# Second layer: a small copy that holds GpSimd's residues behind each routing comparison, and VectorE's residues behind a round's operations

## The chip, the cores and the metric

The kernel runs on one core of one Trainium2 chip. The metric is device time in microseconds (us), the median of several runs. The core has TensorE (PE in the profile, with its weight loads apart as PEld), VectorE (DVE), ScalarE (ACT), GpSimd (POOL) and SyncE (SP, which issues most DMAs). Each engine works its own queue in order; engines wait for each other through semaphores.

## The reference, cut to what matters

Attention with a window makes a matrix x of 3072 rows of 512. A first layer of eight experts follows, and then the second layer, where the change lies. It assigns every row to one of eight experts so that each expert gets 384 rows, then runs the expert's two matrix products:

```python
logits = x @ w_gate
order = np.argsort(-logits.flatten())
for idx in order:
    tok, e = int(idx) // E, int(idx) % E
    if assigned[tok] >= 0 or counts[e] >= cap:   # cap = 3072 // 8 = 384
        continue
    assigned[tok] = e
    counts[e] += 1
out[mask_e] = np.maximum(x[mask_e] @ w1[e], 0.0) @ w2[e]
```

## The kernel before, in words

**The routing.** `Route.steps` doesn't sort. It makes eight picks, k = 0 to 7; each finds the expert that fills next, the score at which it is full, and its 384 rows. A pick of k below 7 runs three or four rounds of a search that narrows the threshold some sixty-fold each time. A round is a chain over two engines. VectorE writes `ub`, then the comparison `cmp` (128 x 1792 numbers, bf16) of all scores with 64 thresholds, then the small numbers `b0` and `b1` (columns of the tile `sc`). TensorE counts the result in 13 small matmuls into the PSUM tile `rt` (L1682). VectorE turns the counts into `gsm` and `gg`, TensorE sums `gg` in one matmul (L1965), and VectorE takes the maximum (`J8m`) and two small operations on `sc`, which start the next round's `ub`. After a pick's last round, VectorE and TensorE (tiles `ohb`, `ft`, `rc`, `pj`) make the list `idx` of the pick's rows, and GpSimd gathers these rows from DRAM (`xg`, three indirect DMAs), followed by a copy of the expert's number (`em`).

**The experts.** `Ffn.run` works the eight picks' experts one after the other, each in eight blocks of the hidden width, 64 blocks in all. Numbers are split in a high part and a residue, so that a product is three matmuls. ScalarE makes the high parts (`w1h`, `w2h`, `hh`, `xh`), and a subtraction makes the residues: `w1l` of the first weights (on VectorE for even blocks, on GpSimd for odd ones), `w2l` of the second weights (always on GpSimd in this layer), `hl` and `xl` on VectorE from PSUM. A block is 12 matmuls into `ph` (L1030) and, two blocks later, nine into `y` (L950). The rows of the next expert are transposed (`tr`, L796) in the blocks 6 and 7 of the one before; `tr` has a single buffer, so that a transposition waits until `xl` of the one before has been read from it. The residues are asked for some blocks ahead: `w1l` three, `w2l` two.

**What sets the order.** The order is written out. In every block `side(q)` is called four times, q = 0 to 3: it issues one of the four splits (0 and 1: the high part and the residue of `w2`; 2 and 3: those of `w1`) and the transpositions that are due, and then calls `tick()`. `tick()` lets the routing (`rt.pop`) issue its next piece if the planner's clocks allow it, and asks for weights and gathers. So the pieces of a routing round come behind a split in each engine's queue.

**The copy that is already there.** In pick 1 alone, GpSimd copies `b0` (one number) to the tile `hold` after each round but the first (L1945 and L1946). Nothing reads `hold`. GpSimd's next instruction starts when the copy is done, and the copy waits for `b0`, which VectorE writes behind the comparison. VectorE writes `b0` of the next round only when the copy has read the one before.

Of the kernel before, what the change touches and what calls it, by code (L numbers as in the profile page):

```python
# [10 lines left out]
F32 = mybir.dt.float32  # L11
# [47 lines left out]
def bc(ap, shape):  # L59
    return ap.to_broadcast(shape)  # L60


class K:
    def __init__(self):
        self.clk = Clock()
# [714 lines left out]
class Ffn:  # L780
# [42 lines left out]
    def run(self, js, w1, w2, src, yout, hook=None, xp=((6, 0), (6, 2), (7, 0), (7, 2)), LEAD=3, LAG=2, pre=None, onx=None, more=(), mark=lambda s, n: None):  # L823
# [5 lines left out]
        total = 8 * len(js)  # L829
# [37 lines left out]
        def poll_w(n, ws=(0, 1)):  # L867
            for _ in range(n):
                for i in ws:
                    w = want[i]  # L870
                    if w and 4 * (w[0] - 1) <= done[i] and (src.ready_e2 if w[0] % 2 else src.ready_e)(alljs[w[0] // 2]):
                        load(i, w.pop(0))
# [19 lines left out]
        def split2(c, part):  # L892
            r, q = need(1, c), c % 4
            if part == 0:
                ch[1][c] = (wk.tile([128, 512], F32R, name="w2h", bufs=W2B),
                            wk.tile([128, 512], F32R, name="w2l", bufs=W2B))
                nc.scalar.activation(ch[1][c][0], r[q // 2][:, q % 2, :] if isinstance(r, list) else r[:, q, :], AF.Copy)  # L897
            else:
                h, lo = ch[1][c]
                eng = nc.vector if self.vsplit or small(c) and c % 2 else nc.gpsimd  # L900
                eng.tensor_tensor(lo, r[q // 2][:, q % 2, :] if isinstance(r, list) else r[:, q, :], h.bitcast(F32), op=OP.subtract)  # L901
                done[1] = c + 1
# [22 lines left out]
        def split(s, part):  # L925
            if part < 2:
                if s in w2at:
                    split2(w2at[s], part)
            elif s + LEAD < total:
                split1(s + LEAD, part - 2)  # L930
# [11 lines left out]
        def tick():  # L942
            if hook is not None:
                hook()
            poll_w(2)
            poll_x()
# [10 lines left out]
        late = []  # L957
# [31 lines left out]
        for s in range(last + 1):  # L989
# [3 lines left out]
            def side(q):  # L993
                while q == 3 and late:
                    split(*late.pop(0))
                if q == 1 and late:
                    late.append((s, 1))
                else:
                    split(s, q)
                if jx + 1 < len(js) and s < total:  # L1000
                    for d in range(4):
                        if xp[d] == (f, q):
                            prep(js[jx + 1], d)
                tick()

            if s < total and small(s):
                q = f % 4
# [453 lines left out]
JC, NIT, FEW, IDLE = 64, 4, 2, (3, 2, 1)  # L1461
# [83 lines left out]
class Route(Src):  # L1545
# [4 lines left out]
    def __init__(self, nc, g, pool, xs):  # L1550
        self.nc, self.g, self.p, self.xs = nc, g, pool, xs
        self.e, self.regs, self.idx, self.x = {}, {}, {}, {}
        self.gen = self.steps()
        self.comp = []
        self.em3 = {}
        self.at = [0.0, 0.0]
        p = pool
        self.L = p.tile([128, NR, E], F32, name="L")
        self.LG = p.tile([128, NSUB, E], F32, name="LG")
        self.ent = p.tile([128, NSUB, 2], I32, name="ent")  # L1560
        self.pn = p.tile([128, NMAIN], F32, name="pn")
        self.vb = p.tile([128, NMAIN], BF, name="vb")
        self.tki = p.tile([128, 3, NMAIN], I32, name="tki")
        self.S_ = p.tile([128, NR], F32, name="S_")
        self.OH = p.tile([128, NR, E], BF, name="OH")
        self.ub = p.tile([128, NR], BF, name="ub")
        self.cmp = p.tile([128, 2, JC, HR], BF, name="cmp")
        self.cuts = ((0, HA), (HA, HT + 1))
        self.cmp2 = [p.tile([128, 2, JC, e - o], BF, name=f"cmp{o}") for o, e in self.cuts]
        self.T = p.tile([128, NR], F32, name="T_")  # L1570
        self.sc = p.tile([128, 20], F32, name="sc")
        self.fl = p.tile([128, E], F32, name="fl")
        self.lb = p.tile([128, E], F32, name="lb")
        self.pad = p.tile([128, SSML], F32, name="pad")
        self.pw = p.tile([128, NIT], F32, name="pw")
        self.dd1 = p.tile([128, 4, NIT], F32, name="dd1")
        self.hold = p.tile([1, 2], F32, name="hold")
        self.of = p.tile([2, 128], F32, name="of")
        self.z = p.tile([128, 64], BF, name="z")
        self.tm = p.tile([128, NR], F32, name="tm")  # L1580
        self.chk = p.tile([128, 3, E], F32, name="chk")
        self.want = p.tile([128, 3, E], F32, name="chw")
        (self.lo0, self.lo, self.lop, self.b0, self.b1, self.J, self.esum, self.eidx, self.bad, self.t0, self.nbig, self.span,
         self.half, self.nrow, self.hi, self.J2, self.nv) = (self.sc[:, i:i + 1] for i in range(17))
# [318 lines left out]
    def steps(self):  # L1903
        nc, g, p = self.nc, self.g, self.p
# [15 lines left out]
        for k in range(E):  # L1920
# [4 lines left out]
            if k < E - 1:  # L1925
# [4 lines left out]
                for it in range(first, last + 1):  # L1930
                    d, inv = dd[:, 0, it:it + 1], dd[:, 1, it:it + 1]
                    if k == 0:
                        if it > first:
                            V.scalar_tensor_tensor(self.ub, bc(dd[:, 2, it - 1:it], [128, NR]), J, self.T, op0=OP.mult, op1=OP.add)
                            self.against(V)
                            V.scalar_tensor_tensor(lo, J, dd[:, 0, it - 1:it], b0, op0=OP.mult, op1=OP.add)
                        if it < last:
                            V.tensor_scalar(b1, dd[:, 3, it:it + 1], lo, None, op0=OP.add)
                            V.tensor_scalar(self.T, S_, b1, dd[:, 1, it + 1:it + 2], op0=OP.subtract, op1=OP.mult)
                        if it == first:  # L1940
                            V.tensor_scalar(b0, d, -1.5, lo, op0=OP.mult, op1=OP.add)
                    else:
                        self.compare(V, slice(0, 2), slice(0, HR), inv)
                        V.tensor_scalar(b0, d, -1.5, lo0 if it == 0 else lo, op0=OP.mult, op1=OP.add)
                        if k == 1 and it > 0:  # L1945
                            nc.gpsimd.tensor_copy(self.hold[:, it - 1:it], b0[0:1])  # L1946
                        if it < last:
                            V.tensor_scalar(b1, dd[:, 0, it + 1:it + 2], -128.0, b0, op0=OP.mult, op1=OP.add)
                    if k == 0 and it == first + 1:
                        z = self.z  # L1950
                    self.fill((0 if k == 0 else WT[7] if k == 1 else WT[0]) if it == first else WT[9 if it == first + 2 else 0] if k == 0 else WT[8])
                    yield clk.dve + CM[min(k, 2)]
                    self.count(pn, range(HT + 1), k == 0 and it > first)
                    clk.mm(64 * (HT + 1))
                    if it == first:
                        nc.tensor.matmul(pc, g.ones, OH, start=True, stop=True, skip_group_check=True)
                        nc.scalar.activation(junk, pc, AF.Copy, accum_out=chk[:, 0, k:k + 1])
                    gg = p.tile([JC, E], BF, name="gg")
                    V.tensor_scalar(gs, pn[JC:2 * JC, E:2 * E], -1.0, float(CAP) - 0.5, op0=OP.mult, op1=OP.add)
                    V.tensor_tensor(gg, pn[0:JC, 0:E], gs, op=OP.is_ge)  # L1960
                    if k == 0 and it > first:
                        V.tensor_scalar(b0, d, -1.5, lo, op0=OP.mult, op1=OP.add)
                    self.fill(WT[1])
                    yield clk.dve + 0.2
                    nc.tensor.matmul(pb, g.ones[0:JC, :], gg, start=True, stop=True, skip_group_check=True)  # L1965
                    V.max(J8, pb)
                    if k == 0 and it == first + 1:
                        nc.tensor.matmul(self.cbank[0:64, 0:64], z, z, start=True, stop=True, skip_group_check=True)
                    if k > 0:
                        if it < last:  # L1970
                            V.scalar_tensor_tensor(lop, J, d, b1, op0=OP.mult, op1=OP.add)
                        V.scalar_tensor_tensor(lo, J, d, b0, op0=OP.mult, op1=OP.add)
# [297 lines left out]
```

## Time and profile before

| | |
|---|---|
| median of 3 runs (lowest to highest) | 872.02 us (867.66 to 873.99) |
| the profiled execution | 868.5 us, of which 866.8 us are its span |
| TensorE busy in the span | 824.1 us (95%) |
| VectorE, ScalarE, GpSimd busy | 612.3, 385.3, 343.3 us |
| mean granted TensorE clock | 0.982 |

The span goes from the first to the last instruction of one execution; times in rows count from its start. The second layer's matmuls begin at 523 us. TensorE is the engine that is nearly always busy, so that its waits and its clock decide the end; the other engines count where TensorE waits for them.

### The profile page before, as it was taken

Reading aid. Unit: us, or ns where it says so; the run is one execution under the profiler, and the core shown is the slowest. Engines: PE = TensorE matmul, PEld = TensorE weight load, DVE = VectorE, ACT = ScalarE, POOL = GpSimd, SP = SyncE. Lnnn points to the kernel's source line nnn. Section 1 sums busy time; section 2 is a strip of 40 time slices with the busy share of each in tenths; the row PEclk is TensorE's granted clock in tenths of the full one; section 3 lists DMA queues with packets and bytes.
Section 4 is the critical chain, followed back from the end, with each engine's and each line's share of the span. In section 5 each row is a group of like instructions: output and inputs, shape, how many; then the busy total and the mean of one; then the engine's idle time right before and its main releaser. Section 6 shows DMA issues by size and latency. Waiting matters only on the chain.

```text
span 866.8 us, 15190 instructions
## 1 busy us (share of the span) xinstructions
PE 824.1 (95%) x5006; PEld 657.6 (76%) x5006; DVE 612.3 (71%) x1760; ACT 385.3 (44%) x1091; POOL 343.3 (40%) x560
## 2 busy tenths in 40 slices
PE   8889999989999999999999988999999898999997
PEld 4666666667888888888888647787888787889995
DVE  6888787866679696969694578776868687753310
ACT  5667777754343434343433213343434252434441
POOL 5456958664230101010000014437374445375562
PEclk9999999999999999999999979999999898999999
DMA  7434645747354535343348125434433444255411
GB/s 214 161 113 142 148 147 147 231 161 215 96 166 126 171 122 164 103 150 119 122 146 309 42 78 180 159 134 134 134 134 135 134 134 135 98 169 172 138 44 42
DMA packets 70655, 122.85 MB, mean 142 GB/s; under 512 B 9890, under 2 KB 24102, under 8 KB 70440
## 3 DMA queue, kind: packets, MB, share of 16 engines
q1 hardware_dynamic: 63848, 102.36, 37.4%
q0 software_dynamic: 6720, 19.43, 7.1%
q8 instruction: 42, 0.69, 0.3%
q14 instruction: 45, 0.37, 0.2%
HBM read 102.06 MB, written 19.71 MB: 140 GB/s over the span
## 4 chain that ended last, share of the span: by engine, by line
PE 75%; DVE 14%; ACT 4%; issue 4%; POOL 1%; DMA 0%; POOLq 0%; DVEq 0%; ACTq 0%
PE ph L1030 27%; PE y L950 27%; PE sp L323 4%; PE po L395 3%; ACT P L352 3%; PE rt L1682 2%; PE tr L796 2%; DVE w1l L922 2%; PE pt L360 2%; PE rc L1517 1%; DVE sc L145 1%; PE px L431 1%; DVE mx L342 1%; DVE cmp L145 1%; PE sp L409 1%
## 5 line engine op out<-in xcount | busy, mean ns | idle before, releaser
L1040 ACT ACTIVATE hh<-ph 128x384 fp32r<-128x384 f32 (+1 forms) x112 | 60.2, 538 | 276.2 <-PE ph L1030 275.6
L1030 PE MATMUL ph<-xh,w1h 128*128 128x384 f32 (+1 forms) x448 | 168.9, 377 | 0.1
L1030 PE MATMUL ph<-xh,w1l 128*128 128x384 f32 (+1 forms) x448 | 162.9, 364 | 2.3 <-DVE w1l L922 2.3
L1030 PE MATMUL ph<-xl,w1h 128*128 128x384 f32 (+1 forms) x448 | 162.1, 364 | 0.0
L950 PE MATMUL y<-w2h,hh 128*128 128x512 f32 x384 | 155.2, 404 | 0.0
L950 PE MATMUL y<-w2h,hl 128*128 128x512 f32 x384 | 151.2, 394 | 0.0
L950 PE MATMUL y<-w2l,hh 128*128 128x512 f32 x384 | 151.2, 394 | 0.0
L1041 DVE SCALAR_TENSOR_TENSOR hl<-ph,hh 128x384 fp32r<-128x384 f32 (+1 forms) x112 | 68.7, 613 | 104.6 <-ACT hh L1040 103.7
L901 POOL TENSOR_TENSOR w2l<-w2r,w2h 128x512 fp32r<-128x512 f32 x60 | 78.0, 1306 | 76.5 <-ACT w2h L897 53.3
L1195 POOL DMA_INDIRECT xg<-xd,ent x26 | 27.8, 1070 | 195.9 <-DMA ent<-idtab 190.6
L1219 DVE SCALAR_TENSOR_TENSOR junk<-yr,wgb 128x512 f32<-128x512 f32 x160 | 103.5, 690 | 0.0
L1030 PEld LDWEIGHTS ph<-xh,w1l 128*128 128x128 f32 x448 | 85.6, 191 | 12.6 <-DVE w1l L922 3.0
L1030 PEld LDWEIGHTS ph<-xh,w1h 128*128 128x128 f32 x448 | 85.7, 191 | 12.0 <-issue 1.7
L352 ACT ACTIVATE P<-sp,mx 128x132 f32<-128x132 f32 x192 | 69.3, 369 | 50.4 <-DVE mx L342 18.0
L1030 PEld LDWEIGHTS ph<-xl,w1h 128*128 128x128 f32 x448 | 85.3, 191 | 7.6
L950 PEld LDWEIGHTS y<-w2h,hl 128*128 128x128 f32 x384 | 72.5, 189 | 15.8
L950 PEld LDWEIGHTS y<-w2h,hh 128*128 128x128 f32 x384 | 73.3, 191 | 11.6
L950 PEld LDWEIGHTS y<-w2l,hh 128*128 128x128 f32 x384 | 72.9, 190 | 11.6
L323 PE MATMUL sp<-kr,qs 64*128 64x260 f32 (+1 forms) x384 | 58.9, 404 | 13.5 <-ACT P L352 12.3
L917 ACT ACTIVATE w1h<-w1r 128x512 fp32r<-128x512 f32 x108 | 67.4, 624 | 3.0 <-DVE lp L449 2.1
L922 DVE TENSOR_TENSOR w1l<-w1r,w1h 128x512 fp32r<-128x512 f32 x78 | 66.5, 853 | 2.4 <-ACT w1h L917 2.4
L897 ACT ACTIVATE w2h<-w2r 128x512 fp32r<-128x512 f32 x108 | 67.6, 626 | 0.0
(392 smaller groups left out, 1398.9 us busy)
## 6 DMA issues: line engine op xcount, KB each, us to landing
w1r<-in_w_dram SPq DMA_DIRECT2D x29, 1024.0 KB, 5.5
w2r<-in_w_dram SPq DMA_DIRECT2D x29, 1024.0 KB, 5.8
vr<-in_v_dram SPq DMA_DIRECT2D x16, 384.0 KB, 4.8
xd<-xb SPq DMA_DIRECT2D x16, 384.0 KB, 3.3
xs<-yr SPq DMA_DIRECT2D x24, 256.0 KB, 5.6
kr<-in_kT_dram SPq DMA_DIRECT2D x15, 396.0 KB, 4.4
qr<-in_qT_dram SPq DMA_DIRECT2D x15, 384.0 KB, 4.8
wgb<-in_wg2T_dram SPq DMA_DIRECT2D x1, 2048.0 KB, 8.9
```

The lines of the kernel that those rows point to most:

```text
L323: nc.tensor.matmul(sp[:, hd, c0:260], qs[o:o + 64, 128 * i:128 * i + 128], kr[o:o + 64, k0:k0 + 260 - c0], start=True, stop=True)
L352: nc.scalar.activation(z.P[:, n % 2, hd, :], s.sp[:, hd, 128:260], AF.Exp, bias=s.mx[:, hd:hd + 1], accum_out=z.sm[:, n % 2, hd:hd + 1])
L897: nc.scalar.activation(ch[1][c][0], r[q // 2][:, q % 2, :] if isinstance(r, list) else r[:, q, :], AF.Copy)
L901: eng.tensor_tensor(lo, r[q // 2][:, q % 2, :] if isinstance(r, list) else r[:, q, :], h.bitcast(F32), op=OP.subtract)
L917: nc.scalar.activation(h, v, AF.Copy)
L922: eng.tensor_tensor(lo, v, h.bitcast(F32), op=OP.subtract)
L950: nc.tensor.matmul(o, l, r, start=(first and i == 0), stop=(end and i == 2))
L1030: nc.tensor.matmul(ph, wp[:, c, :], xp_[:, c, 0:NTK], start=(d == 0 and i == 0), stop=(d == 3 and i == len(cut[d]) - 1))
L1040: nc.scalar.activation(hh, ph, AF.Relu)
L1041: nc.vector.scalar_tensor_tensor(hl, ph, 0.0, hh.bitcast(F32), op0=OP.max, op1=OP.subtract)
L1195: self.nc.gpsimd.indirect_dma_start(out=self.xg[j][:, a, :], out_offset=None, in_=self.G.xd[0:k, :], in_offset=bass.IndirectOffsetOnAxis(a ...
L1219: nc.vector.scalar_tensor_tensor(junk, yr[:, 0:DM], 1.0, wgb[:, e, :], op0=OP.mult, op1=OP.mult, accum_out=lg[:, e:e + 1])
```

## The change

Picks 2 to 6 get the copy too: each round but a pick's first one ends with GpSimd's copy of `b0` to `hold`, which are 14 copies more. And in the second layer, `side(3)` of a block calls `tick()` ahead of its split when that split is one for VectorE (an even `w1` block); the pieces of the routing that this tick issues then stand ahead of `w1l` in the queues.

```diff
             def side(q):
                 while q == 3 and late:
                     split(*late.pop(0))
+                ticked = q == 3 and not self.vsplit and s + LEAD < total and (s + LEAD) % 2 == 0 and not late
+                if ticked:
+                    tick()
                 if q == 1 and late:
                     late.append((s, 1))
                 else:
...
                         if xp[d] == (f, q):
                             prep(js[jx + 1], d)
-                tick()
+                if not ticked:
+                    tick()
...
-        self.hold = p.tile([1, 2], F32, name="hold")
+        self.hold = p.tile([1, NIT], F32, name="hold")
...
                         V.tensor_scalar(b0, d, -1.5, lo0 if it == 0 else lo, op0=OP.mult, op1=OP.add)
-                        if k == 1 and it > 0:
+                        if it > 0:
                             nc.gpsimd.tensor_copy(self.hold[:, it - 1:it], b0[0:1])
```

GpSimd's queue in pick 5, before (`xg` are the gathers of expert 4's rows, the residues those of blocks 26 to 31; pick 6 has the same sequence one expert later, before and now):

```order
L901 TENSOR_TENSOR w2l<-w2r,w2h 128x512
L1882 DMA xg_9009<-xs,idx_9005 128x512 x3
L1885 COPY em_9013<-em 1x1
L922 TENSOR_TENSOR w1l<-w1r,w1h 128x512
L901 TENSOR_TENSOR w2l<-w2r,w2h 128x512 x2
L922 TENSOR_TENSOR w1l<-w1r,w1h 128x512
```

and now:

```order
L901 TENSOR_TENSOR w2l<-w2r,w2h 128x512
L1886 DMA xg_9020<-xs,idx_9016 128x512 x3
L1889 COPY em_9024<-em 1x1
L1950 COPY hold<-sc 1x1
L922 TENSOR_TENSOR w1l<-w1r,w1h 128x512
L901 TENSOR_TENSOR w2l<-w2r,w2h 128x512
L1950 COPY hold<-sc 1x1
L901 TENSOR_TENSOR w2l<-w2r,w2h 128x512
L922 TENSOR_TENSOR w1l<-w1r,w1h 128x512
L1950 COPY hold<-sc 1x1
L901 TENSOR_TENSOR w2l<-w2r,w2h 128x512 x2
```

Three copies have come in: the second one stands between the two `w2l` that followed each other, the third ahead of the pair after that. VectorE's and TensorE's queues are the same before and now in picks 5 and 6.

VectorE's queue in pick 3, where blocks 11 and 12 run, before:

```order
L145 TENSOR_TENSOR ohb<-iob,rb 128x1792
L922 TENSOR_TENSOR w1l<-w1r,w1h 128x512
L145 MEMSET pj 128x2
L145 TENSOR_SCALAR gsm<-rt 64x8
L145 TENSOR_TENSOR gg<-rt,gsm 64x8
L1041 SCALAR_TENSOR_TENSOR hl<-ph,hh 128x384
L145 TENSOR_REDUCE pj<-rc 128x2x3
L145 SCALAR_TENSOR_TENSOR idx_7467<-pj 128x3
L145 SCALAR_TENSOR_TENSOR idx_7469<-pj 128x3
L145 MAX J8m<-rt 128x8
```

and now:

```order
L145 TENSOR_SCALAR gsm<-rt 64x8
L145 TENSOR_TENSOR gg<-rt,gsm 64x8
L922 TENSOR_TENSOR w1l<-w1r,w1h 128x512
L145 MAX J8m<-rt 128x8
L145 SCALAR_TENSOR_TENSOR sc<-J8m,dd,sc 128x1 x2
L145 TENSOR_SCALAR ub<-S__77,sc,dd 128x28
L145 TENSOR_TENSOR cmp<-ub,iou 128x1792
L145 TENSOR_SCALAR sc<-dd,sc 128x1 x2
L1045 SCALAR_TENSOR_TENSOR hl<-ph,hh 128x384
L145 TENSOR_REDUCE pj<-rc 128x2x3
L145 SCALAR_TENSOR_TENSOR idx_7481<-pj 128x3
```

The residue of block 14 stands behind `gg` instead of ahead of it, and the second round's comparison has moved ahead of the row list (`pj`, `idx`) that the gathers read. GpSimd's queue at the same place, before:

```order
L901 TENSOR_TENSOR w2l<-w2r,w2h 128x512 x2
L1882 DMA xg_7471<-xs,idx_7467 128x512 x3
L1885 COPY em_7475<-em 1x1
L922 TENSOR_TENSOR w1l<-w1r,w1h 128x512
L901 TENSOR_TENSOR w2l<-w2r,w2h 128x512 x2
```

and now:

```order
L901 TENSOR_TENSOR w2l<-w2r,w2h 128x512
L1950 COPY hold<-sc 1x1
L901 TENSOR_TENSOR w2l<-w2r,w2h 128x512
L922 TENSOR_TENSOR w1l<-w1r,w1h 128x512
L1886 DMA xg_7505<-xs,idx_7481 128x512 x3
L1889 COPY em_7509<-em 1x1
L1950 COPY hold<-sc 1x1
```

The three gathers, which followed two `w2l`, now follow a copy, a `w2l` and a `w1l`. VectorE's order differs besides in one residue of pick 1 (block 6, which moves behind the second `ohb`) and in pick 4, where two residues and the rounds around them change places; TensorE's order differs in picks 3 and 4 alone, and that of the SP queue nowhere.

## Rows read from the trace of the kernel before

**Rows 1.** Section 1 of the page: TensorE's busy time and share.

```profile
PE 824.1 (95%) x5006; PEld 657.6 (76%) x5006; DVE 612.3 (71%) x1760; ACT 385.3 (44%) x1091; POOL 343.3 (40%) x560
```

**Rows 2.** TensorE's waits, 515 to 867 us: total us, times, longest.

```profile
PE rt L1682 <- DVE cmp L145: 5.6, 2, 3.0
PE tr L796 <- DVE xl L798: 3.2, 3, 1.8
...
PE rc L1517 <- DVE pj L145: 0.5, 1, 0.5
```

**Rows 3.** Timeline, VectorE in pick 5: start, duration, instruction.

```profile
674.76 4.14 DVE L922 TENSOR_TENSOR w1l<-w1r,w1h 128x512 fp32r<-128x512 f32 x1
...
679.02 2.33 DVE L145 SCALAR_TENSOR_TENSOR sc<-J8m,dd,sc 128x1 f32<-128x1 f32 x2
...
681.60 1.09 DVE L145 TENSOR_TENSOR cmp<-ub,iou 128x1792 bf16<-128x1792 bf16 x1
```

**Rows 4.** Timeline, GpSimd at the same place.

```profile
674.59 1.28 POOL L922 TENSOR_TENSOR w1l<-w1r,w1h 128x512 fp32r<-128x512 f32 x1
675.83 2.52 POOL L901 TENSOR_TENSOR w2l<-w2r,w2h 128x512 fp32r<-128x512 f32 x2
678.84 1.28 POOL L922 TENSOR_TENSOR w1l<-w1r,w1h 128x512 fp32r<-128x512 f32 x1 [0.49 <-ACT w1h L917]
```

**Rows 5.** Timeline, VectorE in a round of pick 3 with GpSimd issuing gathers.

```profile
592.66 0.17 DVE L145 MAX8 J8m<-rt 128x8 f32<-128x8 f32 x1 [0.46 <-PE rt L1965]
...
593.47 1.09 DVE L145 TENSOR_TENSOR cmp<-ub,iou 128x1792 bf16<-128x1792 bf16 x1
```

**Rows 6.** Chain that ended last: start, us, what (picks 4, 5 and 6).

```profile
625.71 0.78 PE rt L1682 x13
...
627.78 1.27 PE ph L1030 x6
...
636.10 2.08 PE y L950 x9
...
688.16 2.32 PE y L950 x9
...
734.56 2.95 PE y L950 x9
```

**Rows 7.** Stretches; the number behind the five engines is the granted clock.

```profile
596.00:604.00 8.00, 6.24 (x42) 4.96 (x41) 6.59 (x13) 2.69 (x6) 6.03 (x6) 1.00 0.64 199
...
682.00:689.00 7.00, 6.25 (x30) 5.62 (x31) 4.06 (x13) 0.81 (x2) 0.00 (x0) 0.53 0.38 146
```

**Rows 8.** Timeline, VectorE in pick 6.

```profile
721.56 3.63 DVE L922 TENSOR_TENSOR w1l<-w1r,w1h 128x512 fp32r<-128x512 f32 x1
```

**Rows 9.** Timeline, VectorE and TensorE in pick 2.

```profile
561.88 0.96 DVE L145 SCALAR_TENSOR_TENSOR sc<-J8m,dd,sc 128x1 f32<-128x1 f32 x2
...
565.07 0.55 PE L796 MATMUL tr<-cst,xg 128*128 128x128 f32 x3 [0.64 <-DVE xl L798]
```

**Rows 10.** Timeline, GpSimd's gathers and TensorE's transpositions, picks 2 and 3.

```profile
551.44 0.96 POOL L1882 DMA_INDIRECT xg<-xs,idx  x1 [0.30 <-issue]
...
555.21 0.33 PE L796 MATMUL tr<-cst,xg 128*128 128x128 f32 x1 [0.49 <-DMA xg<-xs,idx]
...
592.40 0.99 POOL L1882 DMA_INDIRECT xg<-xs,idx  x1 [0.63 <-DVE idx L145]
593.69 1.70 POOL L1882 DMA_INDIRECT xg<-xs,idx  x1 [0.30 <-issue]
...
603.79 0.55 PE L796 MATMUL tr<-cst,xg 128*128 128x128 f32 x3 [1.76 <-DVE xl L798]
```

**Rows 11.** Timeline at a copy of pick 1: GpSimd, VectorE, TensorE.

```profile
527.53 0.17 POOL L1946 COPY hold<-sc 1x1 f32<-1x1 f32 x1 [1.68 <-DVE sc L145]
...
527.85 1.65 DVE L922 TENSOR_TENSOR w1l<-w1q,w1h 128x512 fp32r<-128x512 f32 x1
...
529.55 0.45 PE L1030 MATMUL ph<-xh,w1l 128*128 128x384 f32 x1 [1.12 <-DVE w1l L922]
```

## The prediction

> **What bounds the kernel now.** I read the page first: TensorE is busy 824.1 us, 95% of the span [rows 1]. So only its waits and its clock can shorten the time, and the change touches the second layer alone. The view of TensorE's waits from 515 us on shows how little there is: two waits of 5.6 us together for a routing comparison (3.0 and 2.6), three of 3.2 us together for `xl`, and some of half a microsecond [rows 2]. The windows show what belongs to the first two: the granted clock was 0.53 of full speed in the 7 us behind the longer one, while it stayed at 1.00 around the wait of 1.76 us at 603.8 [rows 7, 10]. So the two long waits cost twice, once idle and once at 1.2 instead of 2.4 GHz.
>
> The timeline shows where they come from. In pick 5 VectorE starts a `w1l` at 674.76, takes 4.14 us for it, then 2.33 us for two operations on one number per partition, and the comparison ends at 681.60 + 1.09 = 682.69 [rows 3]. GpSimd runs residues back to back at that very time, one from 674.59 and two until 675.83 + 2.52 = 678.35, then more from 678.84 on [rows 4]. VectorE's residue ends some 0.6 us behind GpSimd's third. Nobody else was late: an undisturbed round takes 593.47 + 1.09 - 592.66 = 1.90 us from the maximum to the comparison's end [rows 5]. VectorE's operations on SBUF stand still while GpSimd works through its residues, and TensorE's count waits for the comparison. Pick 6 is the same with a residue of 3.63 us [rows 8].
>
> **Pick 5, the first term.** The copies put a stop into GpSimd's queue: residue, residue, copy, residue, residue, copy. The first copy stands behind the gathers, while VectorE writes its `b0`, and waits for nothing; it moves GpSimd's first residue by its own length, 0.17 us [rows 11]. From 674.59 + 0.17 GpSimd works two residues (1.28 + 1.26 from rows 4) until 677.3, and then must wait at the second copy for a `b0` that VectorE has yet to write. VectorE is free at 677.3. Its residue needs some 0.6 us more (678.90 behind 678.35 in rows 3 and 4), so 677.9; the undisturbed round of 1.90 us puts the comparison's end at 679.8 instead of 682.7. TensorE was due there at 682.75 - 3.0 = 679.7. A wait of 0.1 us is left of 3.0: **-2.9 us**. If VectorE wins the race at 674.8 and GpSimd's two come behind its residue, they end at 678.0, and the two small operations start then: the comparison ends near 679.6, the same.
>
> With no long wait the clock should not fall. What the fall cost is read off the chain: at full clock, the count and the 12 matmuls behind it took 627.78 + 1.27 - 625.71 = 3.34 us and nine `y` matmuls 2.08 [rows 6]. In pick 5 the same two pieces took 688.16 - 682.75 = 5.41 and 2.32. That is **-2.3 us**.
>
> **Pick 6** has the same queue: the wait of 2.6 us goes whole (GpSimd's two residues end near 723.6, the comparison near 726.2, TensorE is due at 726.5), **-2.6 us**. The slow clock there lasted longer, 2.07 us in the first piece as above and 2.95 - 2.08 = 0.87 in the second [rows 6], **-2.9 us**.
>
> **Picks 1 and 2.** In pick 2 a `w2l` of GpSimd stands behind the first of the new copies, so it can't stretch VectorE's two small operations to 0.96 us, against 0.35 undisturbed; the 0.6 us saved bring `xl` forward and end the wait of 0.64 us [rows 9]: **-0.6 us**. In pick 1 a `w1l` has moved behind the second `ohb`, for which TensorE waited half a microsecond [rows 2]: **-0.5 us**.
>
> **Pick 3, where the change also costs.** The 1.76 us wait for `xl` [rows 10] came from a `w1l` that stood in front of a comparison, and goes. But the gathers of expert 2's rows now stand behind a copy, a `w2l` and a `w1l`, and the list they read behind one more comparison. Worked forward on before's clock: GpSimd's three residues ahead of the copy end near 590.6 and hold VectorE's small operations up to there, the comparison of the second round ends at 592.4 to 592.8, the copy is through at 593.0, the two residues at 595.6 (1.28 each), and VectorE's `idx`, two SBUF operations, may wait for them until 596.0. Three gathers 1.29 us apart (592.40 to 593.69) end at 599.6, and rows land 2.8 us behind the last (555.21 against 551.44 + 0.96) [rows 10]: 602.4. TensorE, which reads them in block 14, is due between 600.2 and 601.5, after up to 1.3 us of waiting for `gg` on the same count. So 1.9 to 2.2 us of new waits replace 1.76: I take **+0.3 us**. Bounds: nothing new at all, -1.8; the gathers one more residue late and a clock fall like that of pick 5 behind it, +1.3 + 2.3 = +3.6.
>
> At this place a rule and a row differ. The second gather took 1.70 us instead of 0.99 while VectorE ran the comparison of 1.09 us [rows 5, 10]. The Trainium skill (SBUF — State Buffer, Who interferes with whom) says that an operation on two SBUF tensors takes only the read side of the ports that VectorE shares with GpSimd, while writing DMA descriptors needs the write side, so the comparison should not have slowed the gather. By the rule the price here would be 0.3 us; should the next comparison slow a gather by the row's 0.7 us, it would be 1.0.
>
> **The rest.** The 14 copies are 14 x 0.17 = 2.4 us of GpSimd, which is 40% busy [rows 1]; they lie beside TensorE's work. Residues held back come up to some 4 us later. They are asked for two or three blocks ahead, a block lasts some 4.2 us (12 matmuls and nine), and no row of TensorE's waits names GpSimd; so 8 us cover 4, at nothing. Behind the third copy of picks 5 and 6 GpSimd's pair now runs against VectorE's next `w1l`, with `gsm`, `gg` and an `xl` queued behind it; by the same reckoning `xl` is just in time: **+0.2 us** for the two, up to +1.3 each if one more residue comes between. Moving the tick ahead of the split adds no instruction; its effect is in picks 1, 3 and 4 above, and pick 4 comes out at nothing within 0.3 us.
>
> **The sum** is -2.9 - 2.3 - 2.6 - 2.9 - 0.6 - 0.5 + 0.3 + 0.2 = -11.3 us. The profiled execution took 868.5 us, so 857.2. Its own before lies 3.5 us under the median of the three runs, 872.02; I take the difference off the median: **860.7 us**. One per cent, 8.7 us, is about what a measurement of this kernel can tell from no change, since the three runs span 6.3 us.
>
> **Rivals.**
>
> The gain is half: the waits of picks 5 and 6 go, but a clock fall stays, because pick 3's wait grows or because a fall hits another weak place. Two falls of the kind in picks 5 and 6 are 2.3 + 2.9 = 5.2 us: -11.3 + 5.2 = -6.1, 866 us, within 1%. For it: the two long waits are not the only ones, and the new one of pick 3 stands beside a count of small matmuls as theirs did. Against it: the wait of 1.76 us was followed by a clock of 1.00 [rows 7, 10].
>
> The copy doesn't hold what matters: the stall may come from the residues in front of the copy, which it leaves where they are. In pick 5 two of three remain ahead of it, and if VectorE needs much longer than 0.6 us to get through behind them, say one GpSimd residue more (1.28 us), a wait of 1.4 us stays in each pick; with the clock staying up, the gain is 11.3 - 2.6 = 8.7 us, 863 us, on the edge of 1%.
>
> The other side: slower. In pick 1, the copy that exists lets GpSimd loose exactly behind the comparison, at 527.53; its `w1l` stretches VectorE's `w1l` to 1.65 us, and TensorE waits 1.12 us for that [rows 11]. If each of the 14 new copies does this, it is 14 x 1.12 = 15.7 us against 11.3: +4.4, 876 us. It decides from 10 of 14 on. For it: VectorE's even residues now stand right behind the round, where GpSimd's start. Against it: pick 1 is the start of the layer, with the residue needed at once; later VectorE's residues are asked for three blocks, 12 us, ahead. The Trainium skill (SBUF — State Buffer, Who interferes with whom) has the rule behind it, that the order of issue decides which of the two blocks the other. The rows agree, 674.59 ahead of 674.76 in pick 5 and 527.53 ahead of 527.85 in pick 1 [rows 3, 4, 11].
>
> **How the numbers follow.** Forecast as worked out (855 to 862.5): 0.58. Copy holds too little (about 863): 0.17. Clock falls stay (about 866): 0.18, with up to 870. Slower by the copies' collisions: 0.04, and 0.03 for no effect at all. The low end is the sum with pick 3 at its good bound (-1.8 for +0.3), 858.6, and as much of the scatter of the runs before, 4.4 us below their median, as chance should leave: 855. The high end takes in the clock falls: 867. Faster by over 1% (under 863.3): 0.68; within 1%: 0.28; slower: 0.04.
>
> **What the profile after would show.** In pick 5 and 6, `w1l` on VectorE takes about 3.1 and 2.5 us, not 4.14 and 3.63; the two small operations behind it 0.35; the count follows with a wait under 0.3 us; the granted clock of both stretches is 1.00. In pick 3 the wait for `xl` is gone and one for `xg` of about a microsecond stands in block 14. GpSimd waits at 14 more copies, and no matmul waits for GpSimd. The prediction is wrong if the comparisons of picks 5 and 6 still end over 1 us late, if the clock falls at new places, or if waits for `w1l` of VectorE appear behind the copies.

## The result, and the profile after

The changed kernel takes 856.56 us (median of six runs, 855.23 to 861.10), against 870.24 us for the kernel before in the same comparison (six runs, 867.66 to 873.99): a ratio of 0.9844, with a 95% interval of 0.9813 to 0.9874. The forecast was 860.7 us in a range of 855 to 867, and faster. The profiled execution took 855.23 us against 868.5, 13.3 us less where the sum of the prediction had 11.3.

Section 1 of the page of the changed kernel, as in [rows 1]:

```profile
PE 818.0 (96%) x5001; PEld 654.6 (77%) x5006; DVE 609.3 (71%) x1760; ACT 385.1 (45%) x1091; POOL 347.5 (41%) x574
```

TensorE's waits of the changed kernel in the second layer, as in [rows 2]: total us, times, longest.

```profile
PE ph L1034 <- DVE w1l L922: 1.1, 1, 1.1
PE tr L796 <- DMA xg<-xs,idx: 0.8, 1, 0.8
...
PE rt L1686 <- DVE cmp L145: 0.5, 2, 0.2
```

The 5.6 us for `cmp` have become 0.5, and `xl`, with 3.2 us in [rows 2], is no longer in the list. No wait names GpSimd. The one for `w1l` is that of pick 1, which was there before [rows 11].

The timeline of VectorE in pick 5 after, to be read against [rows 3]:

```profile
672.97 0.67 DVE L922 TENSOR_TENSOR w1l<-w1r,w1h 128x512 fp32r<-128x512 f32 x1
...
674.34 2.43 DVE L145 SCALAR_TENSOR_TENSOR sc<-J8m,dd,sc 128x1 f32<-128x1 f32 x2
...
677.01 1.09 DVE L145 TENSOR_TENSOR cmp<-ub,iou 128x1792 bf16<-128x1792 bf16 x1
```

GpSimd at the same place, against [rows 4]:

```profile
674.09 1.28 POOL L922 TENSOR_TENSOR w1l<-w1r,w1h 128x512 fp32r<-128x512 f32 x1
675.33 1.29 POOL L901 TENSOR_TENSOR w2l<-w2r,w2h 128x512 fp32r<-128x512 f32 x1
678.29 0.17 POOL L1950 COPY hold<-sc 1x1 f32<-1x1 f32 x1 [1.67 <-DVE sc L145]
678.43 1.28 POOL L901 TENSOR_TENSOR w2l<-w2r,w2h 128x512 fp32r<-128x512 f32 x1
```

GpSimd works its two residues until 676.62, VectorE's small operations are through at 676.77, and the third residue waits 1.67 us at the copy instead of standing in their way. The comparison ends at 678.10. TensorE's count in pick 5, before and now:

```profile
682.75 0.95 PE L1682 MATMUL rt<-OH,cmp 128*128 128x16 bf16 x13 [3.01 <-DVE cmp L145]
...
678.16 0.96 PE L1686 MATMUL rt<-OH,cmp 128*128 128x16 bf16 x13 [0.21 <-DVE cmp L145]
```

It has waited for 0.21 us instead of 3.01. Pick 6 shows the same with `w1l` at 2.26 us (it was 3.63, [rows 8]), and there no wait is left.

Stretches of the changed kernel; the number behind the five engines is the granted clock, as in [rows 7]:

```profile
593.00:598.00 5.00, 5.00 (x20) 4.38 (x19) 2.88 (x10) 0.91 (x2) 4.23 (x7) 0.66 0.56 176
...
676.00:683.00 7.00, 6.79 (x42) 5.55 (x41) 5.71 (x17) 2.81 (x6) 3.65 (x6) 1.00 0.58 165
683.00:690.00 7.00, 7.00 (x48) 5.94 (x47) 4.34 (x11) 2.73 (x6) 4.58 (x4) 1.00 0.36 138
720.00:727.00 7.00, 7.00 (x52) 6.14 (x52) 4.65 (x12) 1.53 (x3) 4.98 (x5) 1.00 0.63 226
```

Behind the counts of picks 5 and 6 the clock stays at 1.00, where it was 0.53 in pick 5. There is one new fall, in pick 3 (0.66).

Where the time went is read from the start of each block's first matmul, before and after. The difference is -1.8 us at block 28, -6.75 at block 30 (pick 5), the same at block 36, -12.3 at block 38 (pick 6), and -12.3 from there to the last block.

### The profile page after: what moved, and what is told of

Its sections match the earlier page's. It is cut to its first block, busy times and chain, and to the rows that moved or that the text cites. A ratio compares the mean times of both kernels' runs of the same rounds, so it can differ in the third digit from the quotient of the medians.

```text
span 853.5 us, 15197 instructions
## 1 busy us (share of the span) xinstructions
PE 818.0 (96%) x5001; PEld 654.6 (77%) x5006; DVE 609.3 (71%) x1760; ACT 385.1 (45%) x1091; POOL 347.5 (41%) x574
## 4 chain that ended last, share of the span: by engine, by line
PE 78%; DVE 10%; ACT 5%; issue 4%; POOL 2%; DMA 0%; POOLq 0%; DVEq 0%; ACTq 0%
PE ph L1034 29%; PE y L950 28%; PE sp L323 4%; PE po L395 3%; ACT P L352 3%; PE tr L796 2%; PE rt L1686 2%; PE pt L360 2%; PE rc L1521 2%; PE px L431 1%; DVE mx L342 1%; DVE cmp L145 1%; PE sp L409 1%; DVE sc L145 1%; DVE sp L340 1%
## 5 line engine op out<-in xcount | busy, mean ns | idle before, releaser
L1034 PEld LDWEIGHTS ph<-xh,w1l 128*128 128x128 f32 x448 | 84.8, 189 | 12.3 <-DVE w1l L922 3.0
L323 PE MATMUL sp<-kr,qs 64*128 64x260 f32 (+1 forms) x384 | 59.1, 405 | 13.3 <-ACT P L352 12.0
L922 DVE TENSOR_TENSOR w1l<-w1r,w1h 128x512 fp32r<-128x512 f32 x78 | 62.9, 806 | 2.4 <-ACT w1h L917 2.4
```

What stands on the lines that cost most here:

```text
L323: nc.tensor.matmul(sp[:, hd, c0:260], qs[o:o + 64, 128 * i:128 * i + 128], kr[o:o + 64, k0:k0 + 260 - c0], start=True, stop=True)
L922: eng.tensor_tensor(lo, v, h.bitcast(F32), op=OP.subtract)
L1034: nc.tensor.matmul(ph, wp[:, c, :], xp_[:, c, 0:NTK], start=(d == 0 and i == 0), stop=(d == 3 and i == len(cut[d]) - 1))
```

## The experiments

Ratios are to the kernel before, run on the same chip beside them (medians 867.46 us for the first four, 867.75 for the others).

**The copies alone.** The kernel before with `if it > 0:` for `if k == 1 and it > 0:`.

> Before with the 14 copies alone, the tick where it was. Theory (the copies hold GpSimd's pair of residues behind the comparison, and that is the gain): the waits for the comparison in picks 5 and 6 are gone as in the changed kernel, with their clock falls, about 10.5 us, and with the earlier xl of pick 2 about 11.5 us come off: ratio 0.986 to 0.989. Pick 3 keeps the old order there, and with it a wait for xl of up to 1.8 us, but no clock fall. Rival (VectorE's own residue in front of a round's operations is what delays the comparison, so that the moved tick matters): under 5 us, ratio over 0.994.

Measured 856.53 us, 0.9864 (0.9816 to 0.9912). The blocks of picks 5 and 6 start 4.9 and 5.6 us earlier, as after the whole change. In pick 3 the wait for `xl` is 0.65 us and the clock doesn't fall; from block 7 to block 16, in picks 2 and 3, the block starts gain another 1.7 us. The copies do the work; the tick isn't needed for it.

**The tick alone.** The changed kernel with `if k == 1 and it > 0:` back in place.

> The moved tick alone, with the copies in pick 1 only as before. Theory: the waits in picks 5 and 6 stay at about 3.0 and 2.6 us with their clock falls, and only the half microsecond of pick 1 and the wait of 1.8 us for xl in pick 3 change, against a clock fall in pick 3 of up to 1.7 us: ratio 0.997 to 1.002. Rival: the moved tick carries the gain, 8 us or more, ratio under 0.991.

Measured 868.12 us, 0.9999 (0.9975 to 1.0024), as the theory had it. Its waits say why:

```profile
PE rt L1686 <- DVE cmp L145: 7.8, 4, 3.0
```

The waits of 3.0 and 2.6 us stand where they were. Of the two others, one of 0.6 us stands in pick 3, and one of 1.6 us ahead of the layer (519.34), which comes and goes between executions: the kernels with one copy in each pick and with the tick moved early have it too. The moved tick alone is worth nothing that can be measured.

**Copies that hold nothing.** The changed kernel, with a constant as the source of the 14 new copies.

```diff
-                            nc.gpsimd.tensor_copy(self.hold[:, it - 1:it], b0[0:1])
+                            nc.gpsimd.tensor_copy(self.hold[:, it - 1:it], b0[0:1] if k == 1 else self.pw[0:1, 0:1])
```

> The changed kernel, with its 14 new copies reading a constant instead of b0: they cost GpSimd their 0.17 us and hold nothing. Theory (holding is what works): in pick 5 GpSimd runs its third residue at once, VectorE's two small operations end some 1.3 us later, and a wait of about 1.4 us for the comparison is back in pick 5 and a similar one in pick 6; 2.6 us without clock falls, some 5 us more with them, so the gain of 13.6 us shrinks to between 6 and 11: ratio 0.987 to 0.993. Rival (a small delay of GpSimd lets VectorE's residue go first, and that is enough): as the changed kernel, ratio 0.984 to 0.985.

Measured 868.95 us, 1.001 (0.9985 to 1.0036): the whole gain is gone, more than either theory said, with four waits for the comparison of 7.0 us together. VectorE in pick 5 of this kernel:

```profile
677.20 4.42 DVE L922 TENSOR_TENSOR w1l<-w1r,w1h 128x512 fp32r<-128x512 f32 x1
...
681.74 1.16 DVE L145 SCALAR_TENSOR_TENSOR sc<-J8m,dd,sc 128x1 f32<-128x1 f32 x2
682.82 1.31 DVE L145 TENSOR_SCALAR ub<-S__77,sc,dd 128x28 bf16<-128x28 f32 x1
684.16 1.09 DVE L145 TENSOR_TENSOR cmp<-ub,iou 128x1792 bf16<-128x1792 bf16 x1
```

And GpSimd:

```profile
677.18 1.27 POOL L922 TENSOR_TENSOR w1l<-w1r,w1h 128x512 fp32r<-128x512 f32 x1
678.42 1.27 POOL L901 TENSOR_TENSOR w2l<-w2r,w2h 128x512 fp32r<-128x512 f32 x1
679.64 0.17 POOL L1950 COPY hold<-pw 1x1 f32<-1x1 f32 x1
679.78 1.28 POOL L901 TENSOR_TENSOR w2l<-w2r,w2h 128x512 fp32r<-128x512 f32 x1
681.24 1.51 POOL L922 TENSOR_TENSOR w1l<-w1r,w1h 128x512 fp32r<-128x512 f32 x1 [0.18 <-ACT w1h L917]
```

A copy that doesn't wait lies between two residues without letting VectorE through: its `w1l` starts 0.02 us behind GpSimd's first residue and ends 0.56 us behind the third, and TensorE waits 3.2 us. The expectation had counted on VectorE's residue going first. Here GpSimd's went first and VectorE's stood, which is called losing the race below. Against the changed kernel, picks 5 and 6 are 10.2 us longer by the block starts, and picks 3 and 4 another 3.8. So it is the waiting of the copy that counts, neither its length nor its place in the queue.

**Six of the 14 copies.** The kernel before with `if (k == 1 or k > 4) and it > 0:`.

> Before with copies in picks 5 and 6 alone (6 of the 14), the tick where it was. Theory: the two long waits and their clock falls go, 10.5 us, and nothing else changes: ratio 0.987 to 0.989. Rival (the copies of the earlier picks are needed, since they set how far GpSimd has got when pick 5 begins): under 6 us, ratio over 0.993.

Measured 857.76 us, 0.9893 (0.9834 to 0.9952), at the upper edge of the theory's range; the block starts gain 10.7 us in the two picks. Here VectorE loses the race in pick 5, and the rows are those that the prediction had worked out (about 3.1 us and 0.35 us):

```profile
674.91 3.09 DVE L922 TENSOR_TENSOR w1l<-w1r,w1h 128x512 fp32r<-128x512 f32 x1
...
678.12 0.35 DVE L145 SCALAR_TENSOR_TENSOR sc<-J8m,dd,sc 128x1 f32<-128x1 f32 x2
```

GpSimd's residue starts at 674.93 here, within 0.02 us of VectorE's, where it came 1.1 us later in the changed kernel. The end of the comparison comes out nearly the same whichever goes first: 5.0 us behind the start of `gg` (674.83) here, 5.2 in the changed kernel.

**The waits filled.** The kernel before, with matmuls that nobody reads in the two long waits.

```diff
                     yield clk.dve + CM[min(k, 2)]
+                    for _ in range({5: 12, 6: 10}.get(k, 0) if it == 2 else 0):
+                        nc.tensor.matmul(self.cbank, g.wz[:, 0:128], g.wz, start=True, stop=True, skip_group_check=True)
                     self.count(pn, range(HT + 1), k == 0 and it > first)
```

> Before, with matmuls that nobody reads ahead of the count in the third round of pick 5 (12) and of pick 6 (10): they fill the waits of 3.0 and 2.6 us for the comparison. Theory (the clock falls because of the idle wait): the waits stay as long in time but TensorE is busy in them, the granted clock stays at 1.00 behind both, and the 2.3 and 2.9 us that the two falls cost come off: 5.2 us, ratio 0.993 to 0.995. Rival (the fall comes from the count's small matmuls, or the fall costs nothing by itself): clock 0.50 behind the counts as before, ratio 0.999 or more.

Measured 865.66 us, 0.9971 (0.995 to 0.9992). TensorE in pick 5 of this kernel:

```profile
680.59 2.76 PE L1954 MATMUL rc<-wz 128*128 128x512 bf16 x12
683.81 0.94 PE L1682 MATMUL rt<-OH,cmp 128*128 128x16 bf16 x13 [0.46 <-DVE cmp L145]
```

And its stretches behind the two counts, against the 0.53 of [rows 7]:

```profile
683.00:690.00 7.00, 6.54 (x45) 5.37 (x44) 4.89 (x14) 1.53 (x3) 1.09 (x1) 1.00 0.39 147
...
730.00:738.00 8.00, 8.00 (x53) 6.81 (x51) 4.29 (x12) 3.76 (x8) 2.03 (x2) 1.00 0.04 13
```

The clock doesn't fall, and the blocks behind start 2.2 us earlier in pick 5 and 2.8 in pick 6, against 2.3 and 2.9 in the prediction. In pick 5 the comparison is as late as before, so that the clock term stands apart from the wait. In pick 6 it doesn't: the comparison ends 1.2 us earlier than before, counted from the start of block 36, so the wait there would have been shorter in any case, and what filling it did for the clock can't be told apart. The median gains less than these 5.0 us, 2.1 us: it misses the theory's 0.993 to 0.995, and the interval reaches 0.995 at its end alone. What the other executions lost isn't settled, since only one has a trace.

**One copy in each of the two picks.** The kernel before with the copy of the third round alone in picks 5 and 6 (`if (it == 2 if k > 4 else k == 1 and it > 0):`).

> Before, with one copy in pick 5 and one in pick 6 (that of the third round), none of the other 12. Theory (only the third residue, which stood between VectorE and its two small operations, has to be held): both long waits and their falls go, 10.5 us, ratio 0.986 to 0.989. Rival (the third copy is needed as well, since without it GpSimd's next pair runs into the small operations of the fourth round): a wait of about 1 us and a clock fall come back in each pick, 3 us each, ratio 0.992 to 0.996.

Measured 860.01 us, 0.9897 (0.9854 to 0.9941), just above the theory's range. Both waits and falls go, 10.6 us by the block starts. In the fourth round GpSimd's free residues stretch the two small operations again (1.58 and 1.15 us in the two picks), but TensorE has other work there and doesn't wait. By the block starts, two instructions of the 14 carry the whole gain of picks 5 and 6. By the medians they are worth 7.7 us; the four runs go from 857.29 to 864.28, and the profiled one enters the layer 4.4 us late (see the last section).

**No copies in pick 1.** The changed kernel with `if k > 1 and it > 0:`.

> The changed kernel without the copies of pick 1, which the kernel before had. Theory of the prediction's rival (a copy lets GpSimd loose right behind a comparison, and its residue then stretches VectorE's): the wait of 1.1 us for w1l at 530 and the 0.6 us for hl ahead of it go, and 1 to 2 us come off the changed kernel, ratio 0.981 to 0.984. The other theory (in pick 1 too, an unheld residue delays the next comparison by more than that): a wait for a comparison of 1 to 3 us appears in the blocks 0 to 5, ratio 0.985 to 0.990.

Measured 860.10 us, 0.9898 (0.9866 to 0.9931): worse than the changed kernel by 4.7 us by the ratios and 3.5 by the medians, though the intervals overlap a little. VectorE and TensorE in pick 1 of this kernel:

```profile
519.01 4.94 DVE L922 TENSOR_TENSOR w1l<-w1q,w1h 128x512 fp32r<-128x512 f32 x1
...
524.40 0.16 PE L1969 MATMUL rt<-gg,ones 64*128 64x8 bf16 x1 [4.12 <-DVE gg L145]
```

GpSimd works three residues from 519.70 to 523.41, and VectorE's residue ends at 523.95: the stall of picks 5 and 6 in a third place. The wait of 1.1 us for `w1l` shrinks to 0.77 us and a wait of 4.1 us appears. The second theory holds, with another wait than it named (`gg`, not the comparison).

This kernel has the changed kernel's queues in pick 3, and its clock doesn't fall there. Its stretch behind the count of block 13, to be read against 593 to 598 of the changed kernel:

```profile
598.50:603.50 5.00, 5.00 (x32) 4.34 (x31) 3.44 (x11) 1.53 (x3) 4.23 (x7) 1.00 0.62 197
```

So the order in pick 3 doesn't by itself make the clock fall.

**The tick moved in blocks 0 to 7 alone.** The changed kernel with `q == 3 and s < 8 and not self.vsplit`.

> The changed kernel with the moved tick only in the blocks 0 to 7 (picks 1 and 2); picks 3 and 4 keep the old order. Theory: the half microsecond of pick 1 and the earlier xl of pick 2 stay, pick 3 goes as with the copies alone, without the clock fall of 1.7 us at 593.5 but with a wait of some 0.7 us for xl: 0.5 us better than the changed kernel, ratio 0.983 to 0.985. Rival (the clock fall in pick 3 isn't tied to the order there): no better, ratio 0.985 to 0.987.

Measured 856.75 us, 0.9854 (0.9826 to 0.9883). The clock doesn't fall in pick 3, and the wait for `xl` there is 0.65 us, as the theory said; against the changed kernel (0.9844) and the copies alone (0.9864) nothing can be told apart. Of the four traces with the moved tick in pick 3, two show the fall (the changed kernel and the copies that hold nothing), of the six without it none; the moved tick may favour it but doesn't set it. No version beat the changed kernel.

## Why the prediction was right, point by point

Forecast, and what the block starts of the two profiled executions show:

| place | forecast, us | measured, us |
|---|---|---|
| pick 5, wait and clock | -2.9 - 2.3 | -2.78 - 2.16 |
| pick 6, wait and clock | -2.6 - 2.9 | -2.76 - 2.80 |
| pick 2 | -0.6 | -0.95 |
| pick 1 | -0.5 | +0.43 - 0.50 |
| pick 3 | +0.3 | -0.69 |
| rest (forecast: the pairs behind the third copies) | +0.2 | -0.12 |
| behind the last block's start | none | -0.92 |
| sum | -11.3 | -13.3 |

**Picks 5 and 6** came as worked out, 10.5 us for 10.7, and the runs with copies there alone, with one copy each, and with copies that hold nothing show that it is the second copy's wait that does it. Nor did it hold too little, as the second rival had it: where VectorE's residue stands (the kernel with six copies), it ends 0.55 us behind GpSimd's second one, 678.00 behind 677.45, for the 0.6 us reckoned. The forecast of the rows held for pick 6 (2.26 us and 0.35) and missed for pick 5, where VectorE's residue went first (0.67 us) and the two small operations stood instead (2.43 us); the prediction had that branch with the same end, and so it was.

**The clock** was the second half of the gain, and it was sized rightly. That the fall follows from the idle wait was shown by filling the wait, cleanly in pick 5 and in one execution's trace.

**Pick 3** is where the sum was off by most. The wait for `xl` went. The wait for `xg` in block 14 didn't come, for two reasons. The gathers ended at 597.61, not 599.6, because the second round's comparison ended at 590.75, 0.5 to 0.9 us earlier than reckoned, once the 1.1 us by which this trace runs ahead are allowed for. VectorE's residue (586.32) had started 0.07 us ahead of GpSimd's (586.39), took 0.67 us and put the comparison forward. And the clock fell at a new place, which the prediction named as a sign of its being wrong. Block 13's matmuls took 596.86 - 592.94 = 3.92 us for the 681.49 - 678.97 = 2.52 of block 29: 1.4 us, by which TensorE came later to the rows. The kernel without copies in pick 1 runs the same queues there without a fall: it does wait for `xg`, 0.68 us in block 14 (606.44) where the prediction named about one, and gains 1.2 us from block 11 to block 16 where the changed kernel gains 0.69. A clock fall at another place is the first rival's mechanism, at a quarter of its price; the order of the change alone doesn't set it.

**Pick 2** gained the 0.6 us forecast and 0.35 more, from a shorter wait for `xl` one block earlier (0.84 to 0.15 us), of which a longer one for `xg` (0.49 to 0.84) took half. **Pick 1** gained its 0.5, and lost 0.4 to a wait for `hl` (0.57 us; 0.14 before) that wasn't forecast; the kernel with six copies, which up to pick 5 is the kernel before, has 0.50, so it is scatter between executions. **At the end**, the granted clock of the last 14 us was 0.98 for 0.88, which gave the last 0.9 us; the same instructions run there, so nothing in the change accounts for it, and that part of the agreement is chance.

**The rivals.** The slower one (each copy lets GpSimd loose on VectorE) was seen in part: VectorE's residues behind the copies at 641.42, 682.94 and 724.30 took 1.65 to 1.66 us each, as in pick 1 [rows 11]. Nobody waited for them, since they are needed three blocks later. And the copies of pick 1, on whose 1.12 us that rival was built, keep off a wait of 4.1 us.

The median forecast, 860.7, stood 4.1 us above the 856.56 measured. Two of these are the sum's, 0.9 of them the chance at the end; most of the rest came from taking the sum off 872.02, the median of three runs, where six runs had 870.24.

## What to carry to other kernels

A wait costs its idle time and what the clock loses behind it; here 5.6 us of waits were worth 10.5 by the block starts. When two engines' elementwise work blocks each other, look for the instruction that a third engine waits for, and let the other engine's queue wait on it with one tiny instruction that reads its result; only the stops that stand ahead of such an instruction pay (here two of 14 brought 10.6 us, and those of picks 2 and 3 some 1.7). Reordering one's own queue did nothing as long as the other engine's queue ran free.

## What was not expected of the hardware

**A gather and the comparison.** A gather of GpSimd that is issued just behind the start of VectorE's comparison stands until it ends; one that is issued ahead of it doesn't. In pick 5 of the changed kernel (GpSimd, with the comparison from 669.33 to 670.42):

```profile
669.41 1.88 POOL L1886 DMA_INDIRECT xg<-xs,idx  x1 [0.16 <-DVE ub L145]
```

And with six copies (the comparison from 671.24 to 672.33):

```profile
671.13 1.00 POOL L1882 DMA_INDIRECT xg<-xs,idx  x1 [0.15 <-DVE sc L145]
```

Among the gathers of picks 3 and 4 in the ten traces, ten that start up to 0.6 us ahead of a comparison take 0.95 to 0.97 us, and thirteen that start while one runs take 1.07 to 1.79 and end some 0.8 us behind its end. So the row that the prediction set against the Trainium skill (SBUF — State Buffer, Who interferes with whom) was no accident: the comparison reads two SBUF tensors and holds a gather. But a gather also reads its list `idx` from SBUF, which the prediction left out; whether that reading or the writing of its descriptors is held, no run here shows. It also goes with who wins the race in pick 5: the first gather is 0.9 us longer in the changed kernel than with six copies, and GpSimd's residue, three gathers later, comes that much later to the race. The copies alone and the one copy in each pick have the long gather (1.88 and 1.87 us) and VectorE's residue first (0.67 us each); the kernels without copies in pick 1 and with the tick moved early have the short one (1.00) and VectorE's residue standing (3.08 and 3.10).

**The loser of the race can stand through several instructions.** VectorE's residue takes 0.67 us alone, 2.26 to 3.60 where it stands through two residues of GpSimd and 3.48 to 4.94 through three, and a copy of 0.17 us between them doesn't let it in. It isn't always so: behind the copies at 682.62 and 723.98 of the changed kernel, VectorE's (1.66 us each) got in behind the first of GpSimd's two. Nor does the start in the rows tell the winner: VectorE's starts 0.02 us ahead of GpSimd's with six copies (674.91, 674.93), and 0.7 us ahead in pick 1 of the kernel without copies there (519.01, 519.70), and stands both times. So the order of the starts, by which the prediction read its rows as agreeing with the rule on the order of issue, doesn't tell the winner here.

**The clock can fall without a wait.** In the changed kernel TensorE is busy 5.00 of 5.00 us in the stretch from 593 to 598 at a granted clock of 0.66, a mean of the full 2.4 GHz and 1.2. Ahead of the fall stand 26 and 13 small matmuls (589.78 to 593.09) of the row list and the count. The kernel without copies in pick 1 has the same order at the same pace, again without a wait, and its clock stayed at 1.00. The tick alone has the same order with a wait of 0.6 us there, and its clock didn't fall either, while with copies that hold nothing, after a wait of 0.7 us, it was 0.57 (593 to 601). What decides stays open.

**Scatter ahead of the layer.** The kernel with six copies and that with one in each pick have the same instructions up to pick 5, yet block 2 starts at 528.09 in the one and at 532.08 in the other. Of these four microseconds, 2.9 are there by the first count of the routing (488.56 and 491.43), well ahead of the layer; the rest comes by the layer's start, with a granted clock of 0.79 and 0.71 from 500 to 524 and a wait of 1.6 us for a comparison that the first one doesn't have. Single executions differ by that much before the change matters, which is why the experiments above are read by block starts.
